# Input loads on two queues, a first block in two halves and a new written order in an attention and mixer kernel

## The chip, the core and the metric

The kernel runs on one core of one Trainium2 chip. The metric is the device time of one execution in microseconds. The names of the engines are those of the profile: PE (TensorE, matrix products), DVE (VectorE), ACT (ScalarE), POOL (GpSimd), and SP (SyncE), whose queue issues the DMA transfers. Results of PE land in eight banks of PSUM and must be copied out by DVE or ACT.

## The reference

The input x has 2048 tokens of 448 features, in bf16. Two layers are added to it:

```
h   = x + attention(layernorm(x), wqkv, wo)      # 16 heads of 28
out = h + mixer(layernorm(h), w_in, w_sp, b_sp, w_out)
```

Attention is local: token t looks at the eight tokens t, t-2, ..., t-14. `wqkv` is one 448 x 1344 matrix whose columns are q, k and v, 448 each. The mixer takes gelu(x w_in), 1792 wide; its second half is normalised and mixed over the tokens with the 2048 x 2048 matrix w_sp, the first half gates the result, and w_out brings it back to 448.

## The kernel before

**Tiling.** Tokens lie in 16 blocks of 128 (`x_tm[:, m]`). For every block m the first layernorm goes: statistics on DVE (`stats`, L673: one BATCH_NORM_STATS2 and one aggregate), `Ln` and `Exp` on ACT for the reciprocal root (`rstd_group`, L708), subtract and scale on DVE (`norm_transpose`, L729), four 128 x 128 transposes on PE, and a copy into `xhT` (features on partitions). Blocks are grouped by four (c = 0 to 3). Group 0 and group 1 are transposed by PE; groups 2 and 3 are normalised on POOL and transposed by DMA. In group 0 every block has its own `Ln` and `Exp`.

The features, 448, are cut into four chunks of contraction: three of 128 rows and one of 64. `wqkv` is loaded into the staging tile `stg` (part of `regW`) chunk by chunk: `load_w` (L582) issues one transfer for the three full chunks and one for the last 64 rows, first for the v columns, then for the q and k columns. The q and k weights are then copied with padding, 28 columns of a head into 32, into `wqp` and `wkp` (`pad_weights`, L612; four copies, two halves each for q and k). `qk_tile` (L758) multiplies a group of 512 tokens by a quarter of the padded q and k weights: eight matmuls into two banks, one copy out. There are 16 such tiles. `v1_block` (L774) does v for one of 19 attention blocks: four matmuls with the staged v weights, one copy. `scores`, `o_block` and `y_block` do the rest of attention, and from about 79 us the mixer runs.

**Order.** Every piece of work is a job with a number (its place in the program text), the engines that may do it, and what it reads and writes. `PLAN` (L64) is a list of all 803 job numbers; its place in the list is a job's rank. `ENGINE` (L102) fixes the engine of the jobs that several could do. `Sched.order` (L250) goes through time by written-down costs and gives each engine the ready job of lowest rank; what comes out is a fixed sequence for each engine, which the engines then follow strictly in order, with semaphore waits between them. For this kernel the sequence of each engine is the order of its jobs in `PLAN`. So an instruction that waits holds up everything behind it on its engine. DMA issues count as jobs of the engine that issues them; here all are on SP.

**Loads.** SP issues: x block 0, x block 1, v weights (three chunks), x blocks 2 and 3, v weights (last chunk), q and k weights (three chunks), q and k weights (last chunk), x blocks 4 to 7, wo in two transfers, x blocks 8 to 11, x blocks 12 to 15. Blocks 4 to 7 wait until the v weights are there, wo and the later x blocks until the first three chunks of q and k are there. POOL's preparation of the masks and of the zeroed padding of later tiles (`iota`, `mf`, `otm`, `Eslot`, L626 to L637) waits for the same.

**The start, engine by engine.** DVE: statistics and norms of blocks 0 to 3, the copy of v tile 0, the copy of xhT2, one padding copy (q, first half), then statistics of nine blocks of groups 1 to 3 with mask steps between them, then the norms of group 1. ACT: the activation table, `Ln` and `Exp` of blocks 0 to 3, copies of xhT0 and xhT1, v tile 1, two padding copies with the copy of xhT3 between them, then copies of q,k and v tiles. POOL has the fourth padding copy. PE fills its waits with 14 matmuls on a tile of ones (`warm`, L654), then: transposes of blocks 0 and 1, v tiles 0 and 1, transposes 2 and 3, v tile 2, q,k tiles 1, 0 and 3 of group 0, v tile 3, q,k tile 2, transposes of group 1, the first scores, v tile 8, and the q,k tiles of group 1.

Of the kernel before, what the change touches and what calls it, by code (L numbers as in the profile page):

```python
# [6 lines left out]
D = 448  # L7
# [43 lines left out]
ADDMASK = (14, 16)  # L51

# [132 lines left out]


class Job:
    __slots__ = ("prio", "num", "ways", "reads", "writes", "deps", "bufs", "ready", "done", "started", "hook", "silent", "dma", "store")


class Sched:
# [922 lines left out]
```

## Time and profile before

| what | us |
|---|---|
| median of three runs (251.82 to 252.85) | 251.84 |
| the profiled execution's own time | 252.46 |
| its span, first to last instruction | 250.7 |
| PE busy in the span | 242.2 |
| DVE busy | 143.4 |
| ACT busy | 90.8 |
| POOL busy | 48.7 |

The span lies 1.76 us under the profiled execution's own time, and that time 0.62 us above the median. Busy times of engines overlap. Matmuls are pipelined, so that the duration of one (379 ns for 512 columns) is longer than the distance from one to the next; a stretch of 23 of them takes 5.34 us. In the prediction a line of the timeline reads: start, duration of the merged piece, engine, line, operation, tiles, count, and in brackets the idle time of the engine before it with what ended it. "SPq" is an issue of a DMA by SP. A line of the table by stretches reads: stretch, its length, then busy time and number of instructions for PE, the weight load of PE, DVE, ACT and POOL, then the granted clock of PE, the mean busy share of the 16 DMA engines and the GB/s they moved.

### The profile page before, as it was taken

The page shows a single profiled execution, that of the slowest core. Times are in us where ns is not written, and L with a number is a line of the kernel's source. Part 1 is how long each engine was busy: PE and PEld are TensorE (multiplying, and loading weights), DVE is VectorE, ACT ScalarE, POOL GpSimd, SP SyncE. Part 2 cuts the span into 40 slices and gives each one's busy share as a digit, 9 for nine tenths or more (in the row PEclk, how much of TensorE's full clock was granted, in tenths as well). Part 3 has the DMA queues.
Part 4 walks back from the last instruction along what each step waited for, and adds up shares of the span by engine and source line. Part 5 has one row for each costly group of instructions (what it writes and reads, how often), then busy time and mean ns, then how long its engine had stood idle before and what let it go on. Part 6 is the DMA issues. An engine that isn't in the chain of part 4 may idle for free.

```text
span 250.7 us, 4263 instructions
## 1 busy us (share of the span) xinstructions
PE 242.2 (97%) x1746; PEld 121.7 (49%) x1769; DVE 143.4 (57%) x296; ACT 90.8 (36%) x105; POOL 48.7 (19%) x97
## 2 busy tenths in 40 slices
PE   7799999999999999999999999999999999999996
PEld 2344545656665544453444444444454454454473
DVE  5779767788989997997522144332351352342343
ACT  4666859887878354577660000000000000000000
POOL 3425230004816058764020000000000000000000
PEclk9999999999999999999999999999999999999999
DMA  6842597885344479868999000000010010011002
GB/s 149 257 144 36 115 305 134 101 99 105 82 84 100 96 201 162 172 128 174 193 186 158 0 0 0 3 0 0 0 54 22 0 42 31 3 37 37 1 3 73
DMA packets 61140, 21.83 MB, mean 87 GB/s; under 512 B 54272, under 2 KB 60480, under 8 KB 61120
## 3 DMA queue, kind: packets, MB, share of 16 engines
q1 hardware_dynamic: 61120, 21.56, 40.9%
q8 instruction: 14, 0.23, 0.4%
q14 instruction: 6, 0.05, 0.1%
HBM read 6.60 MB, written 1.84 MB: 34 GB/s over the span
## 4 chain that ended last, share of the span: by engine, by line
PE 92%; DMA 3%; ACT 2%; SPq 1%; issue 1%; DVE 0%; ACTq 0%
PE psum L1006 38%; PE psum L940 15%; PE psum L762 11%; PE psum L1031 8%; PE psum L779 5%; PE psum L860 5%; PE psum L832 3%; PE psum L946 3%; PE psum L797 3%; DMA regW<-in_A_wqkv_dram 3%; ACT regQ L663 1%; PE psum L747 1%; ACT regE L813 1%; PE psum L804 1%; SPq L565 1%
## 5 line engine op out<-in xcount | busy, mean ns | idle before, releaser
L1017 DVE TENSOR_TENSOR regE<-psum,regE 128x512 bf16<-128x512 f32 (+1 forms) x29 | 19.5, 673 | 68.5 <-PE psum L1006 68.5
L1006 PE MATMUL psum<-regW,regZ 128*128 128x512 bf16 (+1 forms) x235 | 48.9, 365 | 0.3
L1006 PE MATMUL psum<-wspT_lo,regZ 128*128 128x512 bf16 x219 | 48.6, 379 | 0.3
L1006 PEld LDWEIGHTS psum<-regW,regZ 128*128 128x128 bf16 x240 | 23.5, 98 | 25.0
L1006 PEld LDWEIGHTS psum<-wspT_lo,regZ 128*128 128x128 bf16 x224 | 21.9, 98 | 26.4
L813 ACT ACTIVATE regE<-psum 126x1792 bf16<-126x1792 f32 (+3 forms) x19 | 30.5, 1605 | 6.4 <-PE psum L797 5.0
L762 PE MATMUL psum<-xhT,regZ 128*128 128x512 bf16 x118 | 28.1, 379 | 1.4 <-issue 0.5
L734 POOL TENSOR_SCALAR tring<-x_tm,ngm,rst 128x448 bf16<-128x448 bf16 (+1 forms) x32 | 21.3, 678 | 7.1 <-ACT rst L717 4.7
L1031 PE MATMUL psum<-regE,regQ 128*128 128x448 bf16 (+1 forms) x119 | 21.9, 341 | 0.0
L966 DVE BATCH_NORM_STATS2 st<-regZ 128x6 f32<-128x448 bf16 x32 | 19.1, 610 | 4.1 <-ACT regZ L961 3.7
L940 PE MATMUL psum<-w_in,xhT 128*128 128x448 bf16 x96 | 20.2, 353 | 0.0
L674 DVE BATCH_NORM_STATS2 st<-x_tm 128x6 f32<-128x448 bf16 x32 | 18.9, 609 | 2.1 <-DMA x_tm<-in_A_x_dram 1.9
L820 DVE TENSOR_TENSOR regE<-regE,maskb 126x1792 bf16<-126x1792 bf16 (+3 forms) x17 | 18.1, 1063 | 2.7 <-ACT regE L813 2.5
L961 ACT ACTIVATE regZ<-psum 128x896 bf16<-128x896 f32 x16 | 14.6, 917 | 13.4 <-PE psum L940 7.5
L940 PE MATMUL psum<-xhT,w_in 128*128 128x512 bf16 x81 | 18.7, 380 | 0.3 <-issue 0.2
L762 PEld LDWEIGHTS psum<-xhT,regZ 128*128 128x128 bf16 x128 | 11.7, 97 | 14.5 <-DVE pf L641 0.7
L779 PE MATMUL psum<-regW,xhT 128*126 128x448 bf16 (+3 forms) x76 | 17.1, 357 | 1.4 <-DVE xhT L665 0.7
L663 ACT ACTIVATE regQ<-psum 128x1024 bf16<-128x1024 f32 x14 | 14.3, 1023 | 7.4 <-PE psum L762 7.2
L990 ACT ACTIVATE regQ<-psum 128x1024 bf16<-128x1024 f32 x14 | 14.3, 1023 | 6.6 <-PE psum L940 4.5
L1031 PEld LDWEIGHTS psum<-regE,regQ 128*128 128x128 bf16 x119 | 11.6, 98 | 9.8
L1037 DVE TENSOR_TENSOR tring<-psum,x_tm 128x448 bf16<-128x448 f32 (+1 forms) x17 | 10.1, 597 | 8.8 <-PE psum L1031 8.5
L860 PE MATMUL psum<-regW 128*128 128x448 bf16 x64 | 13.9, 352 | 0.0
(76 smaller groups left out, 205.8 us busy)
## 6 DMA issues: line engine op xcount, KB each, us to landing
out_dram<-tring SPq DMA_DIRECT2D x15, 112.0 KB, 1.7
x_tm<-in_A_x_dram SPq DMA_DIRECT2D x3, 448.0 KB, 5.4
w_in<-in_B_w_in_dram SPq DMA_DIRECT2D x1, 1344.0 KB, 7.6
regE<-in_B_w_out_dram SPq DMA_DIRECT2D x1, 784.0 KB, 6.3
regW<-in_A_wqkv_dram SPq DMA_DIRECT2D x1, 672.0 KB, 6.4
regE<-in_B_b_sp_dram SPq DMA_DIRECT2D x1, 512.0 KB, 7.1
w_in<-in_B_w_in_dram SPq DMA_DIRECT2D x2, 224.0 KB, 5.6
regW<-in_A_wqkv_dram SPq DMA_DIRECT2D x1, 336.0 KB, 3.5
```

Source lines behind the costliest of these rows:

```text
L674: dve(prio, 0.61, lambda e: e.bn_stats(lnst[i][:, m, :], x_tm[:, m, :]), [r_x[m]], [r_stat[i][m]])
L734: job(prio, {"pool": (cp, [lambda e, c0=c0, c1=c1, s0=s0: e.tensor_scalar(tring[:, t.slot, c0:c1], x_tm[:, m, s0:s0 + c1 - c0], ngm[i][:, ...
L762: fns = [lambda e, i=i, w=w, c=c: e.matmul(bankcols(b, 512, i), w[:, c, gg, :], xhT[:, c, col0:col0 + 512], start=(c == 0), stop=(c == NCH ...
L779: fns = [lambda e, c=c: e.matmul(bankcols(k, D)[0:nk], xhT[:, c, k0:k0 + nk], stg[:, c, 2 * D:3 * D], start=(c == 0), stop=(c == NCH - 1)) ...
L813: ej = job(prio + 1, {"act": (0.17 + 0.0133 * nq, [lambda e: e.activation(Eheads(b), psum[0:nk, 0:2048].rearrange("p (h c) -> p h c", c=12 ...
L820: job(prio + MP, {by: (cost, [lambda e: e.tensor_tensor(Eheads(b), Eheads(b), maskb[0:nk, mi:mi + 1, 0:nq].to_broadcast([nk, NHEAD, nq]), ...
L860: fns = [lambda e, c=c: e.matmul(bankcols(k, D), OT[:, c, 128 * m:128 * m + 128], wo_sb[:, c, :], start=(c == 0), stop=(c == NCH - 1)) for ...
L940: return [lambda e, i=i, c=c: e.matmul(out(i), lhs(i, c, slice(0, 128)), rhs(i, c, slice(0, 128)), start=(first and c == 0), stop=(not fir ...
L966: dve(prio + 2, 0.61, lambda e, i=i: e.bn_stats(st3[:, m, i, :], z2p[:, m, D * i:D * (i + 1)]), [r_z2p[m]], [r_stat[2][m]])
L1006: fns = [lambda e, s=s: e.matmul(bankcols(k, n), z2p[:, s, fc * 128:(fc + 1) * 128], wsrc[:, s, coff:coff + n], start=(s == 0), stop=(s == ...
L1017: dve(prio + 10, 0.70 * n / 512, lambda e: e.tensor_tensor(ub[:, u.slot, 0:n], bankcols(k, n), bb[:, t0:t0 + n], ALU.add), [k, r_bb], [u])
L1031: fns = [lambda e, fc=fc, k=k, c0=c0, c1=c1: e.matmul(bankcols(k, c1 - c0), z1p[:, fc, 128 * m:128 * m + 128], w_out[:, fc, c0:c1], start= ...
```

## The change

- **Weights.** The four transfers of wqkv on SP become three on ACT's queue: v columns of the three full chunks (336 KB), then the last 64 rows of all columns in one (168 KB), then q and k columns of the full chunks (672 KB). ACT issues the first ahead of its table load, the others behind it.
- **x.** SP issues x0, x1 and x2-3 with nothing between them. Blocks 4 to 7 wait for blocks 2 and 3, no longer for the v weights. wo comes behind the last x blocks.
- **Block 0** is normalised, transposed and copied in two halves (`norm_half`): columns 0 to 255 and 256 to 447. Blocks 2 and 3 share one `Ln` and one `Exp`.
- **Padding copies** may go to POOL in every half; in the new order ACT has q and DVE k of the first half, POOL both of the second.
- **Scratch** of the mask (`mf`, `ij`, `pf`) lies in a part of `regW` instead of tiles of its own.
- `v1_block` becomes `v1_blocks`, which could do two blocks at once; `VPAIRS` is empty, so it does one, as before.
- **Order.** `PLAN` and `ENGINE` are new; the order's costs of loads are too (`share`, one DMA time line for each issuing engine). By `PLAN`, DVE has after the norm of block 1: the padding copy (k, first half), norms 2 and 3, the copy of xhT1, a statistic of block 6, the copy of xhT3, ten more statistics of later blocks, mask steps, and the norms of group 1. ACT has, after the `Ln` and `Exp` of blocks 2 and 3: the padding copy (q, first half), v tile 0, xhT2, v tile 1, q,k tiles 1, 0 and 2, and later the copies of xhT4, xhT5 and xhT6. PE has: transposes of block 0 in halves, v tile 0, transposes 1, 2 and 3, v tile 1, q,k tiles 1, 0 and 2, v tiles 3 and 2, q,k tile 3, transposes 4 and 5, the first scores, transposes 7 and 6, v tile 4, q,k tiles of group 1.

```
 PLAN = (
-    15, 2, 21, 3, 1, 19, 0, 6, 4, 20, 44, 7, 18, 50, 5, 26, 57, 48, 8, 58, 16, 17, 54, 9, 59, 65, 60, 45, 61, 56,
+    4, 2, 18, 3, 0, 1, 14, 7, 20, 51, 8, 19, 46, 25, 17, 5, 43, 6, 15, 50, 16, 57, 56, 45, 58, 67, 48, 59, 60, 44,
...
 ENGINE = {
-    "act": (23, 24, 64, 71, 85, 87, 89, 91, 93, 117, 121, 144, 146, 148, 150, 171, 173, 175, 177, 181, 183, 185,
+    "act": (21, 63, 66, 82, 87, 89, 91, 93, 106, 109, 112, 117, 121, 123, 144, 146, 148, 150, 171, 173, 175, 177,
...
-    "pool": (25,),
+    "pool": (23, 24,),
...
-        dma_free = 0.0
+        dma_free = dict.fromkeys(self.EXEC_ENGS, 0.0)
...
+        mf = regW.buf[:, o_OT:o_OT + 512].bitcast(F32).rearrange("p (k n) -> p k n", k=2)
+        ij = regW.buf[:, o_OT + 512:o_OT + 768].bitcast(I32)
+        pf = regW.buf[:, o_OT + 768:o_OT + 1024].bitcast(F32)
...
-        r_stgqk = [Res("stgqk0"), Res("stgqk1"), r_stgpad]
-        r_stgv = [Res("stgv0"), Res("stgv1"), r_stgpad]
+        r_stgqk = [Res("stgqk0"), Res("stg1"), r_stgpad]
+        r_stgv = [Res("stgv0"), r_stgqk[1], r_stgpad]
...
-        load_x(-100, 0, 1)
-        load_w(-99.5, 392, stg, A_wqkv, QKC, 3 * D, r_stgv)
-        load_x(XONE, 1, 2)
-        load_x(X23, 2, 4)
-        load_w(-98, 784, stg, A_wqkv, 0, QKC, r_stgqk)
-        load_x(-97, 4, 8, r_stgv[:2])
+        load_x(-100, 0, 1, (), 0.65)
+
+        for n, (kb, rows, cols, rs) in enumerate(((336, slice(0, 384), slice(QKC, 3 * D), r_stgv[:1]),
+                                                  (168, slice(384, 448), slice(0, 3 * D), r_stgv[1:2]),
+                                                  (672, slice(0, 384), slice(0, QKC), r_stgqk[:1]))):
+            src = A_wqkv[rows, cols]
+            dst = stg[:, 0:3, cols] if n != 1 else stg[0:64, 3, cols]
+            dma(-99.5 + n, kb, lambda e, src=src, dst=dst, n=n: e.dma_start(
+                dst, src.rearrange("(c p) n -> p c n", p=128) if n != 1 else src), (), rs, "act", 0.65 if n < 2 else 1.25)
+        load_x(XONE, 1, 2, (), 0.65)
+        load_x(X23, 2, 4, (), 0.65)
+        load_x(-97, 4, 8, r_x[2:4])
         load_x(-95, 8, 12, r_stgqk[:1])
         load_x(-94, 12, 16, r_stgqk[:1])
         load_w(-93, 392, wo_sb, A_wo, 0, D, r_wo, r_stgqk[:1])
-        sj = job(-2500, {"act": (1.3, [lambda e: e.preload_act_table_set("natural_log_exp_and_others")])})
-        sj.silent = True
+        first_tables = job(-90, {"act": (1.3, [lambda e: e.preload_act_table_set("natural_log_exp_and_others")])})
+        first_tables.silent = True
...
-            if half == 1:
-                ways["pool"] = (1.0, [lambda e: e.tensor_copy(dst, src)])
+            ways["pool"] = (0.93, [lambda e: e.tensor_copy(dst, src)])
...
+        def norm_half(prio, m, half, c0, c1):
+            t = Buf("t%d_h%d" % (m, half), p_tr)
+            dve(prio, 0.27, lambda e: e.tensor_scalar(
+                tring[:, t.slot, c0:c1], x_tm[:, m, c0:c1], mv[0][:, m, 0:1], rst[0][:, m:m + 1],
+                ALU.subtract, ALU.mult), [r_x[m], r_stat[0][m], r_rstd[0][m], r_trpad], [t])
+            b = Buf("tb%d_h%d" % (m, half), p_bank)
+            fns = [lambda e, c=c: e.transpose(psb[:, b.slot * 1024 + c * 128: b.slot * 1024 + c * 128 + 128],
+                                              tring[:, t.slot, (2 * half + c) * 128:(2 * half + c + 1) * 128], ident[:, :])
+                   for c in range(2)]
+            job(prio + 1, {"pe": (0.15, fns)}, [t, r_trpad, r_ident], [b])
+            copy(prio + 2, (0.28, 0.38), lambda: xhT[:, 2 * half:2 * half + 2, 128 * m: 128 * m + 128],
+                 lambda: psb[:, b.slot * 1024:b.slot * 1024 + 256].rearrange("p (c t) -> p c t", c=2),
+                 [b], [r_xh0 if half else r_xhT[m]])
...
-            step = 1 if c == 0 else 4
-            for lo in range(4 * c, 4 * c + 4, step):
+            for lo, step in ((0, 1), (1, 1), (2, 2)) if c == 0 else ((4 * c, 4),):
...
-                    norm_transpose(base - (10 if c == 0 else -10), 0, m, "pe" if c < XPE else "dma")
+                    norm_transpose(base - (10 if c == 0 else -10), 0, m, "halves" if m == 0 else "pe" if c < XPE else "dma")
```

More of the change, by code (lines that the diff above doesn't have):

```diff
@@ L187 @@
 class Job:
[L188 removed]
+    __slots__ = ("prio", "num", "ways", "reads", "writes", "deps", "bufs", "ready", "done", "started", "hook", "silent", "dma", "store", "at")
 class Sched:
@@ L292, in order @@
                 if j.dma:
-                    dma_free = max(now + 1.9, dma_free) + cost
-                    end, vis = now + 0.45, dma_free
+                    dma_free[e] = max(now + 1.9, dma_free[e]) + cost
+                    end, vis = now + 0.45, dma_free[e]
                 else:
@@ L727, in rstd_group @@
             job(prio, {"pool": (1.0, [lambda e: e.tensor_tensor(T, Y, mhalf[:, lo:hi], ALU.pow)])}, [rc, r_mhalf], r_rstd[i][lo:hi])
+        r_xh0 = Res("xh0")
+        def norm_half(prio, m, half, c0, c1):
[11 more added lines that the diff above has]
+                 [b], [r_xh0 if half else r_xhT[m]])
         def norm_transpose(prio, i, m, by):
+            if by == "halves":
+                for half, (c0, c1) in enumerate(((0, 256), (256, D))):
+                    norm_half(prio, m, half, c0, c1)
+                return
             t = Buf("t%d_%d" % (i, m), p_tr)
@@ L887, in bass_sequential_preLN__sliding_local_dilated__mixer_gmlp__prompt_kernel @@
         for b in range(NAB):
-            v1_block(100 * b + VP if b > 3 else -550 + b, b)
+            if not any(b in p for p in VPAIRS):
+                v1_blocks(100 * b + VP if b > 3 else -550 + b, (b,))
+        for p in VPAIRS:
+            v1_blocks(100 * p[0] + VP if p[0] > 3 else -550 + p[0], p)
         exps = []
```

63 lines of the change are left out of this document (34 added, 29 removed), and 70 rows, old and new, of the table PLAN.

## The prediction

> **What bounds the kernel now.** I read the engine shares first, then the busy time by stretch (the last three columns are the granted clock, the DMA share and GB/s).
>
> ```profile
> span 250.7 us, 4263 instructions
> PE 242.2 (97%) x1746; PEld 121.7 (49%) x1769; DVE 143.4 (57%) x296; ACT 90.8 (36%) x105; POOL 48.7 (19%) x97
> ```
>
> ```profile
> 0.00:12.02 12.02, 8.41 (x41) 3.56 (x42) 7.63 (x21) 6.49 (x15) 4.61 (x20) 1.00 0.72 203
> 12.02:24.00 11.98, 11.37 (x77) 5.68 (x80) 10.26 (x32) 8.60 (x13) 5.17 (x10) 1.00 0.37 97
> 24.00:79.00 55.00, 53.96 (x737) 32.38 (x745) 44.10 (x75) 43.72 (x45) 16.74 (x33) 1.00 0.66 127
> 79.00:130.00 51.00, 50.73 (x325) 23.17 (x329) 39.86 (x96) 30.89 (x33) 22.14 (x36) 1.00 0.80 158
> ```
>
> PE is short of work only at the start: after 24 us it loses 1.04 us and then 0.27 us. Before 12.02 most of its busy time is the warm-up matmul on ones. So a change in the head is worth the time by which the real matmuls come earlier, with as much of them done. The timeline shows what held them back:
>
> ```profile
> 9.74 0.37 SPq L584 DMA_DIRECT2D regW<-in_A_wo_dram  x1
> 10.43 0.95 ACT L616 ACTIVATE regZ<-regW 128x896 bf16<-128x896 bf16 x1 [1.24 <-DMA regW<-in_A_wqkv_dram]
> 11.29 0.58 ACT L663 ACTIVATE xhT<-psum 128x512 bf16<-128x512 bf16 x1
> 12.02 5.34 PE L762 MATMUL psum<-xhT,regZ 128*128 128x512 bf16 x23 [0.37 <-ACT xhT L663]
> 19.79 1.56 DVE L738 TENSOR_SCALAR tring<-x_tm,mv,rst 128x448 bf16<-128x448 bf16 x4
> 23.30 1.67 PE L762 MATMUL psum<-xhT,regZ 128*128 128x512 bf16 x7
> ```
>
> The padding copies wait for the q,k weights until 10.43, and the q,k matmuls start at 12.02. The first three chunks were there at 9.74 (SP waited for them too), the last 112 KB later. Between 12.02 and 19.79 DVE works with short pauses (0.65 and 0.60 us) at the statistics of later x blocks; the second group of q,k tiles starts only at 23.30, behind that work. The same view in stretches for the loads:
>
> ```profile
> 3.00:3.50 0.50, 0.50 (x3) 0.20 (x2) 0.50 (x1) 0.00 (x0) 0.18 (x1) 1.00 0.65 56
> 5.50:6.00 0.50, 0.44 (x6) 0.28 (x5) 0.24 (x2) 0.48 (x1) 0.00 (x0) 1.00 0.93 86
> 6.00:6.50 0.50, 0.24 (x2) 0.00 (x0) 0.50 (x2) 0.44 (x1) 0.00 (x0) 1.00 0.59 149
> 6.50:8.50 2.00, 1.56 (x9) 0.96 (x9) 1.33 (x5) 1.04 (x5) 0.00 (x0) 1.00 1.00 355
> 10.00:10.50 0.50, 0.00 (x0) 0.00 (x0) 0.45 (x2) 0.07 (x1) 0.44 (x3) 1.00 0.10 34
> ```
>
> **The change, part by part.** Let p be the start of the first padding copy, 10.43 us now.
>
> *Loads.* SP issues x0, x1, x2-3 back to back, and ACT the weights in three transfers. Together they are 1624 KB, 1.66 MB; now x4-7 (448 KB, issued at 6.93) share the DMA engines too, so 2.12 MB move from about 1.9 us to 10.0, 260 GB/s on average. That average has holes (56, 86, 149 GB/s) beside 355. Upper rate: 355 throughout, if the second queue fills the holes. Then the weights' last byte is there at 1.9 + 1.66/0.355 = 6.6, and p = 7.0, since now 0.4 us lie between the end of the traffic at 10.0 and the copy at 10.43. Lower rate: 260. Then 8.3 + 0.4, and x4-7, now tied to x2-3 alone, begin to flow near 7.5 and take up to half of the rest: p = 8.7 to 9.7, say 9.2. I take the upper rate: the holes lie where one transfer of SP's row of issues gives way to the next, and two queues seldom stand there at once.
>
> *ACT.* It issues 3 DMAs (0.43, 0.56 and 0.58 us by SP's rows for such transfers) around its table load (1.28): 0.79 to 3.64. The first Ln comes at 3.81 now and, with x0 sharing the engines with the v weights (112 KB more, 0.3 to 0.4 us), at about 4.1: nothing lost. If an issue costs ACT up to twice as much, 1.6 us more, Ln of x0 is late by 1.1, and that is behind p all the same unless p falls under 8. SP loses four issues (2.07 us), which brings x2-3 out at 1.7 instead of 2.18.
>
> *Floor by x.* At 355 GB/s x2-3 land at 4.9. DVE then has the two half norms of block 0 (0.39 now; 0.4 to 0.78 in two), two statistics at 0.61, two aggregates at 0.17 and norm 1 at 0.39: done at 7.4. The padding copy of k stands behind these in DVE's order, so p = 7.4, not 7.0. The halves cost PE nothing (four transposes as before) and ACT one copy more (0.58 to 1.27 for the two), ahead of 7.4, where ACT idles. One Ln and Exp for blocks 2 and 3 saves ACT 0.49, also there.
>
> *What DVE now does behind p.* This part speaks against the change: norms 2 and 3, the copies of xhT1 and xhT3 and one statistic stand behind the padding copy. Copy 0.38, norms 0.78, xhT1 0.42, a statistic 0.6, xhT3 0.42: the first q,k matmul at p + 2.75 with its semaphores, against 10.43 + 1.59 now, and with v tile 2 (0.76 us of PE) still to do. After that, to the first norm of block group 1: ten statistics (6.0), eleven aggregates (1.87) and four small steps of the mask (0.30, 0.41, 0.33 and some 0.4): p + 12. Norm 0.39, transpose 0.35, three copies in a row on ACT (0.59 each, held by the norms): the second q,k group starts at p + 14.7, against 10.43 + 12.87 now. PE has the same tiles done at that point in both orders. So the lead is 23.30 - (p + 14.7) = 8.6 - p: 1.2 us for p = 7.4, none at 8.6, a loss behind it.
>
> *POOL.* It takes a second padding copy: its list behind the weights ran 9.78 to 14.16, plus 0.93 is p + 5.3; the third q,k tile wants it at p + 2.75 + 3.4 = p + 6.2. Hidden, with 0.9 to spare. The mask scratch lies elsewhere: no instruction changes.
>
> *The order behind it.* Of 16 blocks' statistics two more (1.55 us of DVE with aggregates) are done before the second group instead of between 22 and 29 us. PE's losses from 22 to 34 (0.09, 0.05 and 0.16 by stretch) are what that can give back: 0.3. The rest of the new order is a reshuffle of equal work: from all later losses recovered (0.8 more) to 1.0 worse, taken at 0.
>
> *Sum.* 1.2 + 0.3 = 1.5. The profiled execution took 252.46 (span 250.70, 1.76 around it) and becomes 250.96; it stands 0.62 above the median of three, 251.84. Forecast for the median: **250.3 us**. Half a per cent (1.26 us) is about what a measurement tells here from no change.
>
> **Rule against row.** The Trainium skill, page "DMA: Bandwidth & Descriptors", section "Issuing engines are not separate DMA queues", says that transfers from different engines run on the same 16 DMA engines and that issuing from several saves only sequencer time. By that rule the average would stay, which is the first rival's time. The DMA share of 1.00 at 355 GB/s agrees with it, the share of 0.59 and 0.65 at the holes does not.
>
> **Rivals.**
>
> *The rate stays (0.18).* For it: the DMA share is 0.93 to 1.00 in most of the stretch, one of the holes included. Against: the holes at 3.0 and 6.0. Then p = 9.2, 0.6 late: 252.4 with no credit for the order.
>
> *Slower: DVE stands at the padding copy (0.14).* If the q,k weights come no earlier than now, because x4-7 and the x blocks share with them to the end, everything DVE has behind the copy waits with it: p = 10.43 gives 8.6 - 10.43 = 1.8 lost, 253.7. It decides from p = 9.9 (1.26 lost). For it: x4-7 no longer wait for a weight, and x8-15 are issued as soon as the q,k weights land. Against: 0.46 MB less have to move first.
>
> *The new order waits more later (0.09).* From 24 to 79 us DVE and ACT are busy 80% each, so a tile that is late by one copy shows in PE at once. If PE's losses after 24 us went from 1.3 to 4.0, a lead of 1.2 would become a loss of 1.5: 253.3; it decides from 2.5 more than now. Against: before has only 1.3 there under an order made in the same way, and the work per engine is the same.
>
> *PE slows down in the head (0.04).* The warm-up matmuls start 0.43 us apart up to 4.8 us, and the same shape goes at 0.23 after 12.02. Now no idle stretch of PE in the head is over 0.75 us; in the new order PE has little between transpose 1 (7.6) and transpose 2 (p + 0.9). If the slow rate came back for 3.2 us, 1.6 us of matmuls would be lost: 251.9.
> The Trainium skill, "TensorE: Matmul & The Clock Gate", Part 1, puts the return to half rate at an idle window of some 3.4 us; a gap of 0.7 to 2 us would not do it alone.
>
> **How the numbers follow.** The forecast's case has 0.55: p from 7.0 to 8.4 and the order from 0.8 better to 0.5 worse, 249.4 to 251.5; 0.40 of it lies under 250.58, 0.15 above. With the rate that stays (0.18) and the slow PE (0.04), both within 0.5%, and the two slower ones (0.14 and 0.09): faster 0.40, same 0.37, slower 0.23. The range leaves out the best of the first case and the upper part of the slower ones: 249.4 to 253.2; the forecast's own is 249.4 to 251.5.
>
> **What would show it.** Right: the first padding copy near 7.4 us, no 0.5 us stretch under 200 GB/s between 2.5 and 6.5, the first q,k matmul near 10.2, the second group near 22.1, PE's loss after 24 us no larger than 1.3. Wrong: a DVE wait for the weights in front of the padding copy that ends after 8.6; a long wait of ACT's first Ln; matmuls of the first q,k tile 0.43 us apart; losses of PE after 24 us of 2 us or more.

## The result, and the profile after

The changed kernel takes 252.78 us (median; 252.24 to 253.50) against 251.96 (251.47 to 252.91) for the kernel before beside it: a ratio of 1.0028, 95% interval 1.0015 to 1.0041. That is inside half a per cent, and on the slow side: 250.3 was forecast, 1.5 less than before, and 0.8 more came out. The profiled execution of the changed kernel took 252.58 with a span of 250.8; that of before, 252.46 with 250.7, lies 0.5 above its own median, so this pair of traces shows only 0.1 of the 0.8, and the trace of before is the one that is not typical: a typical execution of it is half a microsecond shorter. A second trace of the changed kernel (below) has a span of 251.5.

The same view as before in stretches; the columns are the stretch, its length, busy time and instructions of PE, its weight loads, DVE, ACT and POOL, the granted clock, the DMA share and GB/s.

```profile
0.00:11.29 11.29, 9.06 (x37) 3.82 (x38) 7.53 (x20) 5.52 (x12) 5.63 (x22) 1.00 0.75 227
11.29:24.00 12.71, 12.05 (x81) 6.21 (x83) 11.39 (x35) 8.76 (x15) 5.59 (x9) 1.00 0.39 82
24.00:79.00 55.00, 54.02 (x746) 32.65 (x754) 42.86 (x71) 44.59 (x45) 18.66 (x33) 1.00 0.62 129
79.00:130.00 51.00, 50.51 (x323) 22.99 (x326) 41.12 (x97) 30.28 (x32) 21.72 (x35) 1.00 0.90 160
```

The first q,k matmul starts at 11.29, 0.73 earlier than before. After 24 us PE loses 0.98 and 0.49 us, in all 0.2 more than before. The loads in the same view, the stretch from 2.5 to 7.0 and two behind it:

```profile
2.50:7.00 4.50, 3.67 (x12) 1.31 (x11) 2.72 (x8) 1.55 (x7) 0.64 (x4) 1.00 1.04 339
7.00:7.50 0.50, 0.50 (x2) 0.10 (x1) 0.50 (x3) 0.28 (x1) 0.00 (x0) 1.00 0.32 75
7.50:8.00 0.50, 0.50 (x3) 0.27 (x2) 0.50 (x5) 0.19 (x1) 0.02 (x1) 1.00 0.78 116
```

The second queue does fill the holes up to 7.0: 339 GB/s on average, against 222 over the same nine half microseconds before. Then come two stretches of 75 and 116 GB/s. The timeline of the head, PE first, then DVE and POOL (a last line of PE in these views can be cut off where the view ends; the first group of q,k tiles runs on):

```profile
1.40 3.59 PE L662 MATMUL psum<-warm 128*128 128x512 bf16 x8 [1.40 <-POOL warm L579]
5.83 0.39 PE L745 MATMUL psum<-ident,tring 128*128 128x128 bf16 x2 [0.83 <-DVE tring L741]
7.50 1.70 PE L814 MATMUL psum<-regW,xhT 128*128 128x448 bf16 x4
9.42 0.85 PE L776 MATMUL psum<-ident,tring 128*128 128x128 bf16 x12
10.35 0.97 PE L814 MATMUL psum<-regW,xhT 128*126 128x448 bf16 x4
11.29 2.75 PE L791 MATMUL psum<-xhT,regZ 128*128 128x512 bf16 x12
...
4.66 0.63 DVE L682 BATCH_NORM_STATS2 st<-x_tm 128x6 f32<-128x448 bf16 x1 [0.62 <-DMA x_tm<-in_A_x_dram]
7.97 0.79 DVE L626 COPY regZ<-regW 128x896 bf16<-128x896 bf16 x1
8.69 0.84 DVE L767 TENSOR_SCALAR tring<-x_tm,mv,rst 128x448 bf16<-128x448 bf16 x2
9.87 0.42 DVE L673 COPY xhT<-psum 128x512 bf16<-128x512 bf16 x1 [0.34 <-PE psum L776]
10.74 0.41 DVE L673 COPY xhT<-psum 128x512 bf16<-128x512 bf16 x1
19.58 2.37 DVE L767 TENSOR_SCALAR tring<-x_tm,mv,rst 128x448 bf16<-128x448 bf16 x4 [0.34 <-ACT rst L731]
...
7.98 0.54 POOL L643 MEMSET otm<- 128x512 bf16 x1 [4.76 <-DMA regW<-in_A_wqkv_dram]
```

Four things are to be seen. The padding copy starts at 7.97 (7.4 was forecast), as soon as the weights are there: POOL waited for the same transfer until 7.98. DVE was not free much earlier either, since its norm of block 1 had started only at 7.69. Block 1's statistic waits for x block 1 until 4.66, where it began at 3.69 before, and the half norms of block 0 now stand behind it; so the first transpose comes at 5.83, and PE idles for 0.83 us between the warm-up and it. Behind that gap the four matmuls of v tile 0 take 1.70 us; 0.92 is what such four take later in the same trace, so PE goes at about half the rate. The granted clock reads 1.00 all the while, so this rate is read from the distance between matmuls alone. And the group 1 norms took 2.37 us in place of 1.56.

### The profile page after: what moved, and what is told of

The parts are those of the page before. It is cut to its first block, busy times and chain, and to the rows that moved or that the text cites. A ratio compares the mean times of both kernels' runs of the same rounds, so it can differ in the third digit from the quotient of the medians.

```text
span 250.8 us, 4268 instructions
## 1 busy us (share of the span) xinstructions
PE 243.5 (97%) x1746; PEld 122.7 (49%) x1769; DVE 144.6 (58%) x296; ACT 90.4 (36%) x104; POOL 51.6 (21%) x98
## 4 chain that ended last, share of the span: by engine, by line
PE 87%; DVE 8%; ACT 1%; DMA 1%; issue 1%; SPq 0%
PE psum L1044 38%; PE psum L978 11%; PE psum L791 10%; PE psum L1069 8%; PE psum L814 6%; PE psum L896 4%; PE psum L868 3%; DVE tring L767 2%; PE psum L984 2%; PE psum L833 2%; DVE st L1004 2%; DMA x_tm<-in_A_x_dram 1%; PE psum L662 1%; DVE st L682 1%; DVE x_tm L899 1%
## 5 line engine op out<-in xcount | busy, mean ns | idle before, releaser
L814 PE MATMUL psum<-regW,xhT 128*126 128x448 bf16 (+3 forms) x76 | 17.9, 368 | 0.0
L671 ACT ACTIVATE regQ<-psum 128x1024 bf16<-128x1024 f32 x15 | 15.4, 1024 | 6.5 <-PE psum L791 6.3
L1028 ACT ACTIVATE regQ<-psum 128x1024 bf16<-128x1024 f32 x14 | 14.3, 1024 | 6.8 <-PE psum L978 4.6
```

Source lines behind the costliest of these rows:

```text
L814: fns = [lambda e, c=c, i=i, k0=k0: e.matmul(bankcols(k, D, i)[0:nk], xhT[:, c, k0:k0 + nk], stg[:, c, 2 * D:3 * D], start=(c == 0), stop= ...
```

## The experiments

For each run the table gives, from its one trace, when block 1's statistic starts (with the new loads that is the landing of x block 1; in before the block had landed at 3.34, and DVE came to it at 3.69), the first q,k matmul, the time from there to the first mixer matmul, from that to the first matmul of the token mix, and the span; beside them the medians. The ratio is that to the kernel before run beside it, whose median was 251.96 to 252.39, and need not be the quotient of two medians. What follows the token mix takes the same time in all of them (the span less that landmark is 120.5 to 120.6).

In every edited kernel but before_gap three more lines in `Sched.order` make each engine take its jobs strictly as the list has them, so that an edit moves nothing but what it names.

| kernel | block 1's statistic | first q,k | q,k to mixer | mixer to token mix | span | median us | ratio to before |
|---|---|---|---|---|---|---|---|
| before | 3.69 | 12.02 | 67.23 | 50.90 | 250.7 | 251.96 | 1 |
| before_again | 3.59 | 11.88 | 67.23 | 50.90 | 250.6 | one, 252.3 | |
| after | 4.66 | 11.29 | 67.88 | 51.09 | 250.8 | 252.78 | 1.0028 [1.0015, 1.0041] |
| after_again | 5.18 | 11.45 | 68.12 | 51.35 | 251.5 | 253.21 | 1.0044 [1.0032, 1.0056] |
| loads_only | 4.70 | 12.83 | 67.23 | 50.90 | 251.5 | 253.03 | 1.0018 [0.9998, 1.0039] |
| loads_norm0 | 4.94 | 12.97 | 67.23 | 50.90 | 251.7 | 252.92 | 1.0023 [1.0003, 1.0042] |
| loads_warm | 4.73 | 10.99 | 67.24 | 50.90 | 249.7 | 251.50 | 0.9981 [0.9970, 0.9991] |
| loads_warm_again | 5.14 | 11.47 | 67.24 | 50.93 | 250.2 | 251.97 | 0.9993 [0.9977, 1.0009] |
| before_gap | 3.66 | 12.31 | 67.23 | 50.90 | 251.0 | 252.43 | 1.0015 [1.0002, 1.0028] |
| after_warm | 4.92 | 10.75 | 67.89 | 51.35 | 250.6 | 252.64 | 1.0021 [1.0007, 1.0035] |
| after_table_first | 4.83 | 10.73 | 67.89 | 51.09 | 250.3 | 252.96 | 1.0017 [0.9995, 1.0040] |
| after_norm0 | 5.13 | 11.07 | 68.03 | 51.18 | 250.9 | 252.64 | 1.0016 [1.0001, 1.0030] |
| after_stats | 5.38 | 11.18 | 67.77 | 51.06 | 250.6 | 252.95 | 1.0020 [1.0000, 1.0041] |
| after_both | 4.92 | 11.42 | 67.64 | 51.33 | 251.0 | 252.50 | 1.0027 [1.0012, 1.0042] |
| after_mixorder | 5.16 | 11.12 | 67.90 | 50.92 | 250.5 | 252.91 | 1.0035 [1.0018, 1.0051] |
| after_three | 4.93 | 11.29 | 67.97 | 51.48 | 251.3 | 252.90 | 1.0030 [1.0015, 1.0046] |
| all_mended | 5.21 | 11.50 | 67.89 | 51.80 | 251.8 | 252.78 | 1.0024 [1.0009, 1.0039] |
| before_mixorder | 3.64 | 11.33 | 67.24 | 51.18 | 250.3 | 252.81 | 1.0017 [0.9993, 1.0041] |
| after_head | 5.00 | 11.87 | 68.81 | 50.89 | 252.1 | 253.77 | 1.0057 [1.0036, 1.0078] |
| before_head | 3.58 | 11.97 | 69.33 | 51.05 | 252.9 | 255.21 | 1.0129 [1.0106, 1.0153] |

The row "after" is the pair of the result. Executions of one kernel differ by 1 us and more (before: 251.03 to 254.57 over all its executions), so a term of 0.3 us is read from the traces, and a median confirms only the larger ones. A trace can lie far from its own median: after_table_first has a span of 250.3, but its traced execution took 252.00 where its median is 252.96.

The most telling column is the fourth. It rests on two landmarks, here the first mixer matmul of before and then of the changed kernel:

```profile
79.25 1.30 PE L940 MATMUL psum<-w_in,xhT 128*128 128x448 bf16 x6
79.17 1.30 PE L978 MATMUL psum<-w_in,xhT 128*128 128x448 bf16 x6
```

With the attention order of before, the first mixer matmul follows the first q,k matmul by 67.23 or 67.24 us in every trace (the two hybrids with a seam in that stretch apart), whatever the loads, the matmul rate in the head or DVE did: group 1's norms began anywhere from 18.29 to 20.26, 7.29 to 7.82 behind that start. So everything in the head acts through one number, the start of the first q,k matmul. That start itself moves in the kernel before: 12.02, 11.88, 11.97 and 11.33 in four traces with its head (the last two are before_head and before_mixorder), because the q,k weights let the padding copy start anywhere from 9.76 to 10.43. With the changed order the stretch takes 67.6 to 68.1 (the hybrid again apart): one v tile fewer (0.76 us of PE) lies in front of that start and has to be done behind it. The size fits; no run moved that tile alone.

**The same two kernels again.** No edit.

> The kernel before, unchanged, for a second profile. All theories: span 249.7 to 251.2, first q,k matmul at 11.8 to 12.2, second group of q,k tiles at 23.1 to 23.5. Theory C (the matmul rate in the head depends on an unbroken warm-up): the first v tiles at about 0.21 us a matmul again, since the warm-up runs on without a break to 4.8 us; if they go at 0.43 here, the rate changes from run to run in this kernel too.

> The changed kernel, unchanged, for a second profile and as control: ratio 1.0015 to 1.0041. Theory A (the start: what the earlier weights gain is used up before 23.3 us by waits of DVE): first padding copy at 7.8 to 8.2, a DVE wait for x blocks 8 to 11 that ends near 13.2, second group at 23.2 to 23.5. Theory B (the later order costs the time): second group at 23.2 to 23.5 and PE's losses after 24 us above 1.31 us by 0.5 or more. Theory C (the warm-up is broken at 5.0 us, and the matmul rate stays low for longer): v tile 0 at 0.43 us a matmul.

Before repeats to 0.14 us. The second trace of the changed kernel has the first q,k matmul at 11.45 and needs 0.24 and 0.26 us more in the two stretches behind it. In it v tile 0 took 0.92 us and not 1.70, behind a gap of 1.44 us: a slow PE comes and goes between executions of one kernel, and is not what makes the changed kernel slower in this one. Here the padding copy started at 8.44, when the weights came; DVE had waited 0.36 us for them.

Why x block 1 comes later can be read from the traces. In the first one of the changed kernel the DMA queues moved, from 2.5 to 3.5 us (queue, packets, MB, share of the engines' time; q10 is ACT's queue, q1 that of SP):

```profile
q10 hardware_dynamic: 333, 0.30, 90.6%
q1 hardware_dynamic: 29, 0.02, 5.9%
```

In that microsecond the v weights had the engines almost alone, and x block 1, issued at 1.24, stood behind them. In before SP's one queue moved 0.13 MB in it, and the block was there at 3.34.

**The loads alone.** The kernel before with the new loads and its own order of computing; ACT's first weight transfer stands ahead of the table load, as in the changed kernel.

```diff
 load_x(-100, 0, 1)
-load_w(-99.5, 392, stg, A_wqkv, QKC, 3 * D, r_stgv)
+load_qkv(slice(0, 384), slice(QKC, 3 * D), r_stgv[:1])
+load_qkv(slice(384, 448), slice(0, 3 * D), r_stgv[1:2])
...
-load_w(-98, 784, stg, A_wqkv, 0, QKC, r_stgqk)
-load_x(-97, 4, 8, r_stgv[:2])
+load_qkv(slice(0, 384), slice(0, QKC), r_stgqk[:1])
+load_x(-97, 4, 8, r_x[2:4])
```

> The kernel before with the three weight transfers on the other queue and x4-7 behind x2-3; the order of all computing is that of before. Theory A: the loads are a gain and the order spends it. The padding copy comes at about 8.2 instead of 10.43, the order of DVE has the statistics of blocks 4 to 7 first, so it does not wait for blocks 8 to 11; the second group of q,k tiles at 21.3 to 22.0 instead of 23.3, the time 0.8 to 1.8 us under before, ratio 0.993 to 0.997. Theory B: the same gain. Rival (the x loads behind the weights set the pace of the statistics whatever the order): second group at 23.0 or later, ratio 0.999 to 1.001. Theory C: no statement on the loads, but if v tiles 0 and 1 go at 0.43 us a matmul the gain is 0.3 to 0.8 less.

The expected gain did not come. The twelve executions fall into two groups: 251.39 to 252.21 (five) and 253.03 to 253.69 (seven). The one trace is of the second group; its PE:

```profile
1.65 3.17 PE L663 MATMUL psum<-warm 128*128 128x512 bf16 x7 [1.65 <-POOL warm L578]
5.90 0.61 PE L756 MATMUL psum<-ident,tring 128*128 128x128 bf16 x4 [1.08 <-DVE tring L747]
7.58 3.19 PE L788 MATMUL psum<-regW,xhT 128*128 128x448 bf16 x8
12.83 1.46 PE L771 MATMUL psum<-xhT,regZ 128*128 128x512 bf16 x6
```

A gap of 1.08 us behind the warm-up, then v tiles 0 and 1 in 3.19 us; 1.67 is what they took before. DVE's copy of v tile 0 stands ahead of its norms of blocks 2 and 3 in this order, so the slow tiles delay these and with them the q,k tiles.

**The loads alone, with the warm-up kept.** Three more warm-up matmuls ahead of the first transpose, nothing else; run twice, on two chips.

```diff
-job(1e8, {"pe": (0.37 * WARMJ, [lambda e: e.matmul(psum[:, 0:512], warm[:, 0:128], warm[:, :])] * WARMJ)},
+more = WARMJ + 3 * (i == 3)
+job(1e8, {"pe": (0.37 * WARMJ, [lambda e: e.matmul(psum[:, 0:512], warm[:, 0:128], warm[:, :])] * more)},
```

> The loads-only kernel with three more warm-up matmuls ahead of the first transpose, nothing else. Theory that the slow PE behind the 1.08 us gap makes the upper group of its executions: the gap falls under 0.3 us, v tiles 0 and 1 take 1.67 us in place of 3.19, all executions lie in 251.3 to 252.4, median 251.4 to 251.9, ratio 0.9965 to 0.9990. Rival, that the two groups come from the loads (which of the two queues gets the engines first): still two groups, median above 252.4, ratio 1.001 or more.

> The same kernel as loads_warm, beside the next two. If its gain is real: median 251.3 to 251.9, ratio 0.996 to 0.9992, second q,k group at 22.0 to 22.6 us. If it was the chip or the time: ratio 1.000 or more.

```profile
1.65 4.45 PE L664 MATMUL psum<-warm 128*128 128x512 bf16 x10 [1.65 <-POOL warm L578]
5.93 0.40 PE L757 MATMUL psum<-ident,tring 128*128 128x128 bf16 x4
7.15 1.68 PE L789 MATMUL psum<-regW,xhT 128*128 128x448 bf16 x8
10.99 5.34 PE L772 MATMUL psum<-xhT,regZ 128*128 128x512 bf16 x23
```

This is the first of the two runs. The gap is gone, the v tiles take 1.68, the upper group of executions is gone (251.36 to 252.21), and the kernel is faster than before: 0.9981. Its median, 251.50, is that of the lower group before, 251.48. In the traces the lead of 1.03 us at the first q,k matmul is carried to the end unchanged (span 249.7 against 250.7). The repetition gave 251.21 to 252.66 and 0.9993; block 1 landed 0.41 later there and a gap of 0.26 us came back, with the first transposes slow again. Both fall on the same side; the second interval holds no gain as well, so how large it is (nothing to 0.3%) is left open.

**The gap closed in another way.** The loads alone, with DVE's norm of block 0 (job 62) ahead of block 1's statistic (job 65), and the warm-up as it was.

```diff
-rest = [n for n in PLAN if n not in (4, 5, 8, 9, 15)]
+rest = [n for n in PLAN if n not in (4, 5, 8, 9, 15, 62)]
+rest.insert(rest.index(65), 62)
```

> The loads-only kernel with DVE's norm of block 0 ahead of block 1's statistic, so that the first transpose doesn't wait for x block 1; no more warm-up. Theory of the slow PE: first transpose at 4.6 to 5.1 us, PE idle ahead of it under 0.3 us, v tiles fast, one group of executions, median 251.3 to 251.9, ratio 0.9965 to 0.9990. Rival of the loads: two groups, median above 252.4.

```profile
5.08 0.61 PE L756 MATMUL psum<-ident,tring 128*128 128x128 bf16 x4 [0.26 <-DVE tring L747]
6.90 0.61 PE L756 MATMUL psum<-ident,tring 128*128 128x128 bf16 x4 [0.79 <-DVE tring L747]
7.73 3.19 PE L788 MATMUL psum<-regW,xhT 128*128 128x448 bf16 x8
```

The expectation missed: the gap only moves. The first transpose comes at 5.08, but the second, which needs x block 1, leaves PE idle for 0.79 us, and the v tiles are slow all the same. The executions lie from 251.51 to 253.68 again. What counts is not where the first transpose stands but whether PE has a break before it is at the fast rate. Over all twenty traces, v tile 0 was slow in five of the nine in which PE idled 0.74 us or more ahead of a transpose between the warm-up and v tile 0, and in none of the other eleven.

**The gap alone.** The kernel before, two of its first seven warm-up matmuls cut from 512 to 16 columns.

```diff
+w = 16 if i in (3, 13) else 512
-... [lambda e: e.matmul(psum[:, 0:512], warm[:, 0:128], warm[:, :])] * WARMJ)},
+... [lambda e, w=w: e.matmul(psum[:, 0:w], warm[:, 0:128], warm[:, 0:w])] * WARMJ)},
```

> The kernel before with two of the seven warm-up matmuls ahead of the first transpose cut from 512 to 16 columns, so that PE stands idle for 0.8 us there; loads and order unchanged. Theory of the slow PE: v tiles 0 and 1 at 0.43 us per matmul in all or some executions, which are 1.0 to 1.6 us longer: a median of 252.6 to 253.7, or two groups that far apart. Rival, that a gap of 0.8 us does nothing or that the slow v tiles are hidden: one group, ratio 0.999 to 1.001.

```profile
4.83 0.61 PE L748 MATMUL psum<-ident,tring 128*128 128x128 bf16 x4 [0.82 <-DVE tring L739]
6.51 3.19 PE L780 MATMUL psum<-regW,xhT 128*128 128x448 bf16 x8
12.31 5.34 PE L763 MATMUL psum<-xhT,regZ 128*128 128x512 bf16 x23 [0.23 <-ACT xhT L664]
```

The slow rate is there without any change of the loads: a gap of 0.82, then v tiles at 3.19. The cost is not (median 252.43, ratio 1.0015, 252.6 or more was expected). In this trace the padding copy waited for the q,k weights until 10.73, and the first q,k matmul followed 1.58 behind it, as in before (1.59): the 0.29 by which it is later comes from the weights, and the slow tiles are hidden in front of them. What the small rise of the median comes from is open. In the loads-only kernel the weights come early and the same slow tiles lie open: there ACT waited 1.94 us for v tile 1 ahead of its padding copy at 11.25, and the middles of that kernel's two groups, 251.48 and 253.15, are 1.7 us apart.

**The changed kernel with its warm-up kept, and two other edits of its head.** Two more warm-up matmuls; or the table load (job 14) ahead of ScalarE's first weight transfer (job 4); or the half norms of block 0 (61, 64) ahead of block 1's statistic (67).

```diff
+more = WARMJ + 2 * (i == 10)
```
```diff
-    4, 2, 18, 3, 0, 1, 14, 7, 20, 51, 8, 19, 46, 25, 17, 5, 43, 6, 15, 50, 16, 57, 56, 45, 58, 67, 48, 59, 60, 44,
+    14, 2, 18, 3, 0, 1, 4, 7, 20, 51, 8, 19, 46, 25, 17, 5, 43, 6, 15, 50, 16, 57, 56, 45, 58, 67, 48, 59, 60, 44,
```
```diff
-    ... 45, 58, 67, 48, 59, 60, 44, 68, 61, 69, 52, 9, 64, ...
+    ... 45, 58, 61, 64, 67, 48, 59, 60, 44, 68, 69, 52, 9, ...
```

> The changed kernel with two more warm-up matmuls ahead of the first transpose, which fill PE's idle stretch of 5.0 to 5.8 us; nothing else. Theory C: v tile 0 at 0.21 us a matmul (0.9 us instead of 1.7), the first q,k matmul near 10.9 instead of 11.29, the time 0.3 to 0.8 us under the changed kernel, ratio to before 0.9995 to 1.0015. Theory A: v tile 0 may be faster, but DVE still waits for x blocks 8 to 11 near 13.2, the second group stays at 23.1 to 23.4 and the ratio at 1.002 to 1.004. Theory B: ratio unchanged, 1.0015 to 1.0041.

> The changed kernel with ACT's table load ahead of its first weight transfer, so that the v weights start to flow some 1.3 us later; nothing else is moved. Theory A1 (the weights on the second queue take the DMA engines from x0 and x1, so that the first norm is late and the warm-up breaks off): x1 lands at 3.6 to 4.2 instead of 4.66 to 5.18, PE's idle stretch ahead of the first transpose shrinks from 0.8 to 1.4 us to under 0.4 us. The v weights land about 1 us later; first q,k matmul 0.2 to 0.5 earlier than in the changed kernel or equal, ratio to before 1.000 to 1.003. Rival (x1 is late because a queue takes its own time for each transfer): x1 at 4.6 or later again, ratio 1.002 to 1.006.

> The changed kernel with DVE's two half norms of x block 0 ahead of block 1's statistic; nothing else moves. Theory that the head breaks because the first transpose stands behind a statistic that waits for x block 1: first transpose at 4.8 to 5.1 us, PE idle ahead of it under 0.4 us, v tile 0 at 0.23 us per matmul, second q,k group at 22.6 to 22.9, ratio 1.000 to 1.0015. Rival, that the lateness of the x blocks themselves decides: transpose 1 stays where it was (after 6.4 us), second q,k group at 23.2 or later, ratio 1.002 to 1.003.

In all three v tile 0 runs at the fast rate (0.92 us), and the first q,k matmul comes 2.88 to 2.90 behind the padding copy, where the slow execution of the changed kernel needed 3.32 and the one with a fast v tile 0 needed 3.01: a slow v tile 0 costs 0.3 to 0.4 there. The padding copy itself started at 7.87, 7.83 and 8.19, with the weights. The medians, 252.6 to 253.0, do not tell these kernels from the changed one; the shorter times that were expected are not shown. The table load turned out not to hold the transfers up at all: the first weight transfer left at 0.82 against 0.79, and block 1 landed at 4.83, so this run did not test what delays it (the queues' shares above do).

**The statistics of group 1 and POOL's norms.** A statistic of block 5 (96) ahead of those of blocks 11 and 8 on DVE, and ScalarE's `Ln` and `Exp` of group 1 ahead of those of group 2; then this with the two more warm-up matmuls.

```diff
-    ... 94, 23, 95, 130, ... 126, 96, 184, ... 97, 133, 152, 158, 102, 37, 134, 38, 103, ...
+    ... 94, 23, 95, 96, 130, ... 126, 184, ... 97, 102, 152, 158, 103, 37, 133, 38, 134, ...
```

> The changed kernel with two moves in the order: the statistic of block 5 ahead of those of blocks 11 and 8, and on ACT both steps of group 1 (Ln, Exp) ahead of those of group 2. Theory A2 (DVE waits 0.65 to 1.1 us for blocks 8 to 11, and the norms of group 1 on DVE then run beside POOL's norms and take 2.38 us instead of 1.56): DVE's wait shrinks by 0.6, two of the four norms are done before POOL starts, second group of q,k tiles at 22.3 to 22.8 instead of 23.3 to 23.5, time 0.5 to 0.9 under the changed kernel, ratio 0.9995 to 1.0015. Theory B (the later order): the second group earlier, but the time unchanged, ratio 1.002 to 1.0045.

> As after_three, but with the changed kernel's own order from the first mixer matmul on. If that order costs the 0.15 to 0.45 us that the stretch showed: 51.05 to 51.35 us in the stretch, and 0.1 to 0.5 us above after_three, ratio 0.998 to 1.0010. If it does not: the same median as after_three within 0.1.

The norms of group 1 are back at 1.56 us (2.05 in the second), and the second q,k group starts 11.55 us behind the first in place of 12.03. Half of that is not real: in the trace of the changed kernel, as in that of before, the record of this group's first matmul is missing, so that its start is read 0.23 us late (in after_table_first it is there, and the distance is 11.81). The gain is 0.25 us; the v tile just ahead of the group says the same (10.70 behind the first q,k matmul, 10.95 without the edit). Of it 0.1 to 0.25 is left at the first mixer matmul (67.77 and 67.64), and nothing is seen in the medians.

**The order from the first mixer matmul on.** At that point the two orders hold the same work but for one job, so they can be exchanged there: before with the later order of the changed kernel, the changed kernel (warm-up kept) with that of before, and two combinations: with the table load and half norms moved (all_mended), and with the warm-up and the statistics (after_three).

```diff
-order = PLAN
+order = PLAN[:405] + [n for n in OTHER if n not in PLAN[:405]]
```

(`OTHER` is the other kernel's `PLAN`; the engines of the jobs behind the cut are taken from it too. In the kernels the resulting list is written out.)

> The kernel before with the changed kernel's order from just ahead of the first mixer matmul on (the two orders hold the same work done at that point but for one job); loads, head and attention as before. Theory that the later order itself costs: first mixer matmul to first token-mix matmul takes 51.05 to 51.35 us as in every run with that order so far (50.9 before), and the ratio to before is 1.0006 to 1.0018. Rival, that the stretch is longer only because the changed head and attention hand over another state of the engines: 50.9 us again, ratio 1.000.

> The changed kernel with two more warm-up matmuls (as in the run so named) and, from just ahead of the first mixer matmul on, the order of before. Theory that the later order costs: 50.9 us from the first mixer matmul to the first token-mix matmul in place of 51.35, and a ratio of 1.0003 to 1.0010 in place of 1.0021. Rival: the stretch stays at 51.05 to 51.35 and the ratio at 1.002.

> The changed kernel with three mends together: ScalarE's table load ahead of its first weight transfer, the half norms of block 0 ahead of block 1's statistic, and the order of before from the first mixer matmul on. If head and later order are the two causes and add up: second q,k group at 22.0 to 22.6 us, 50.9 us from first mixer to first token-mix matmul, ratio 0.9965 to 0.9995. If something else eats the gains: second q,k group below 22.7 and still a ratio of 1.001 or more.

> The changed kernel with its warm-up kept (two more matmuls), the statistic and ScalarE's steps of block group 1 ahead (as in after_stats), and the order of before from the first mixer matmul on. Theory that these three terms are the whole loss: second q,k group at 22.2 to 22.6 us, 50.9 us from first mixer to first token-mix matmul, median 251.4 to 252.0, ratio 0.997 to 0.9995. Rival, that something else of the new head or of the attention's order costs (seen as more than 56.0 us from the second q,k group to the first mixer matmul, or a second group behind 22.6): ratio 1.000 to 1.002.

The first two traces agree with a cost of the later order: 51.18 with it behind the head of before, 50.92 without it behind the changed head. The combinations do not: 51.80 and 51.48 with the order of before, and both missed the gain that was expected of them. There PE loses most of it in one place, here in all_mended (the waits of PE in that stretch: for what, us in total, times, longest):

```profile
PE psum L897 <- issue: 0.7, 1, 0.7
PE psum L834 <- ACT regE L850: 0.3, 1, 0.3
```

It is a product with wo, in front of which the profile shows no releaser; DMA transposes of its operand were issued 2.6 us ahead, and whether it waits for these was not tried. So the stretch is 0.15 to 0.45 us longer in every trace that ran the changed order there, but longer still in two of the four that ran the order of before behind the changed head: that the later order itself costs is not shown, and why the stretch differs stays open. The four medians (252.8 to 252.9) do not settle it, and after_both, with the changed order there, was expected above after_three, with that of before, and came out below (252.50 and 252.90 on one chip).

**Two hybrids cut further ahead**, the changed head with the rest of before (cut behind the transposes of group 1) and the reverse.

> The changed kernel up to the transposes of group 1, then the order of before for all jobs that are left (v tile 4 moved behind that point with them). Theory B (the new later order loses time between 79 and 130 us, 51.1 to 51.35 there instead of 50.90): the stretch from the first mixer matmul to the first token-mixing matmul is 50.9 again, ratio 0.3 us lower than the changed kernel, 1.000 to 1.002. Theory A: the stretch makes no difference, ratio 1.0025 to 1.0045.

> The kernel before, loads and head unchanged, with the changed kernel's order for the jobs behind the transposes of group 1. Theory B: first mixer matmul to first token-mixing matmul takes 51.1 to 51.4 instead of 50.90, and the time is 0.2 to 0.6 us over before, ratio 1.001 to 1.0025. Theory A: ratio 0.999 to 1.0005.

Both are slower than either kernel for a reason of their own, which is argued: at the cut an engine's list waits for what the other order would have done earlier. In before_head it is one wait of PE:

```profile
PE psum L780 <- ACT xhT L664: 2.0, 1, 2.0
```

They say little of the change, except that the stretch behind the first mixer matmul went with the order that ran there (50.89 and 51.05).

## Why the prediction was wrong

The sum was -1.2 (the lead of the second q,k group) and -0.3 (the later order). In the first trace the two came to 0.0 and +0.1, in the second to +0.2 and +0.6. The step that failed is the lead, 8.6 - p with p = 7.4. In the first trace 0.57 of the 1.2 went because the padding copy came at 7.97, 0.57 because the first q,k matmul came 3.32 behind it and not 2.75, and 0.08 from there to the second group; in the second trace 1.04, 0.26 and 0.09. Besides, the 10.43 us from which the lead was counted belongs to an execution 0.5 us longer than the median of before, and the sum took the 0.62 off in full afterwards.

**Loads, the upper rate: right up to 7.0 us, wrong at the end.** 355 GB/s was taken, 339 came, and the second queue filled the holes: no stretch between 2.5 and 6.5 lies under 200. The last byte was put at 6.6; at 7.0 there were 0.03 MB of the weights left, and these needed until about 7.5. All traffic then went at 75 and 116 GB/s, and the copy came at 7.97 and 8.44. x4-7, issued at 6.40, are not what held the end up in the first trace: from 7.0 to 7.5 the engines were busy for 0.32 of their time with everything. What makes the last bytes slow stays open.

**Floor by x: the first part of p that failed.** "x2-3 land at 4.9" was worked out from the bytes in front of them. With the weights on a second queue x block 1 landed at 4.66 and 5.18 and x2-3 at 6.41 in the first trace, not earlier than before (3.34 and 5.83) but later: from 2.5 to 3.5 us the weights issued beside them had 0.30 of the 0.32 MB that moved. A sum over both queues cannot say which block lands when. The floor put DVE at 7.4; it came to the copy at 7.97, when the weights came too.

**What DVE does behind p: the sum right, two sizes off.** The first q,k matmul was put at p + 2.75; 2.88 to 3.14 came with a fast PE, 3.32 with the slow one. The padding copy took 0.79 and not 0.38, the wait for a slow transpose 0.34. From there to the second group 11.95 was forecast and 12.03 came, which is luck: the path was another one. Not DVE's statistics held the norms of group 1, but ACT's `Exp`, for which DVE idled 0.34 us ahead of them (the line at 19.58). On ACT it stands behind copies of PE's tiles, and the norms began 8.29 or 8.30 us behind the first q,k matmul in all eight traces with the changed order up to there and the statistics where it has them. The stretch itself is 11.28 before and 12.03 or 12.04 with one v tile more behind the first q,k matmul (both read 0.23 late, as said above). DVE is not without weight in it: the norms of group 1 in 1.56 us in place of 2.37 took 0.25 off. The v tile had been named, and with a fast PE the lead of 8.6 - p comes out within about 0.2: 0.73 by it for the padding copy at 7.87 in after_warm, 0.51 measured.

**The order behind it: sign wrong.** 0.3 was credited; 0.1 was gained up to the first mixer matmul in the first trace (55.95 to 55.85 from the second group), 0.1 lost in the second, and the stretch behind it took 0.19 and 0.45 more. What the 0.3 was to come from, statistics done earlier, no run separates. The rival *new order waits more later* was right in kind and far too large (2.7).

**PE slows down in the head: named, and dismissed for a wrong reason (0.04).** The gap was looked for between transposes 1 and 2; it opened ahead of the first. And of two rules the wrong one was set against it. The Trainium skill, "TensorE: Matmul & The Clock Gate", Part 1, gives an idle window of some 3.4 us for falling back to half rate, but also a busy window of that length, running on its own time, for leaving it, with an onset that differs between executions. PE had not yet left it when the gap came. The traces agree with the second half: fast matmuls began 3.6 us after the gap in the changed kernel, some 4.9 in the loads-only one and 5.1 in before_gap, and in other executions of the changed kernel a gap did no harm. The price had been 1.6 us; the slow tile cost 0.3 to 0.4 in the changed kernel, and about 1.7 in the loads-only one. No run here shows a fall back from the fast rate.

**The rate stays** forecast 252.4, near what came, but that is luck: the rate did not stay, 339 against 222 GB/s. **DVE stands at the padding copy** did not happen; the copy came 2.0 to 2.5 us earlier than before.

**The account.** In the changed kernel's two traces the first q,k matmul comes 0.73 and 0.57 earlier, the v tile behind it and the attention's order take 0.65 and 0.89, the mixer's stretch 0.19 and 0.45: +0.11 and +0.77, as the spans have it. Against a typical execution of before, 0.5 us shorter than its trace, the picture is simpler. An estimate: if that half microsecond lies ahead of the first q,k matmul, as the fixed stretches behind it say, the typical start there is 11.5, the changed kernel leads by only 0.1 to 0.2, and gives back 0.84 to 1.34 behind it, that is 0.6 to 1.3 us lost where the medians have 0.8. The v tile and the rest of that loss were not tested one by one, and none of the mended versions of the changed kernel won it back. The loads by themselves, with the warm-up kept, gained 0.19% and 0.07%, the second of these not clear of zero. The rest of the change (order, halves, padding copies) takes that back: beside each other on one chip, loads_warm_again and after_both gave 251.97 and 252.50. Of all that ran, the loads with the order of before and three more warm-up matmuls were fastest.

## What to carry to other kernels

Before pricing an earlier transfer, find the one start through which the head acts on the rest, and count what must still be done behind it: here 2.5 us at the padding copy became 0.7 at the first q,k matmul and 0.1 at the first mixer matmul. Count also what a second queue makes later: the small transfers that share the engines with it. In this kernel the warm-up was safe only when it ran without a break up to the first real work, so whatever moves that work later needs more of it. And look whether the trace from which a lead is counted is a typical execution: here the one of before was 0.5 us long, which is a good part of the lead.

## What was not expected of the hardware

Behind a break of PE of 0.8 to 1.2 us, before it had reached the fast rate, matmuls went at half the rate for 3.6 to 5.1 us more, in some executions and not in others of the same kernel, with a granted clock of 1.00 throughout. One kernel's executions fell into two groups 1.7 us apart; the trace of the slower one has the slow tiles, and that the faster one has none is inferred.

DVE's copies and norms took between once and twice their time: the padding copy 0.38, 0.58, 0.79 and 1.07 us in different kernels, the four norms of group 1 1.56 to 2.38. POOL was busy beside the long ones, but in before its norms also ran beside DVE's, for 1.0 us, and these took 1.56; overlap alone does not explain it, and it was not taken further.

The time from the first q,k to the first mixer matmul repeated to 0.01 us over eight traces in which the loads and the matmul rate in the head differed.
